# A fused attention and two-layer expert kernel: converting the second layers' weights two steps behind their load, every fourth step

## The chip, the cores and the metric

The kernel runs on one core of one Trainium2 chip. The metric is device time in microseconds (us) of one execution. The core has TensorE (PE, with its weight loads shown as PEld), VectorE (DVE), ScalarE (ACT), GpSimd (POOL) and SyncE (SP), which issues the DMAs. Each engine works through its own queue in order, so an instruction that waits holds up all that is queued behind it on that engine.

## The reference

Everything is computed in fp32.

```python
q_s = softmax(q, axis=-1); k_s = softmax(k, axis=2)        # 8 x 8 heads, 576 tokens, 64 wide
x = q_s @ (k_s.T @ v)                                      # per head, then heads side by side: 4608 x 512
h = x @ moe_w_in;  g = maximum(0.01 * h, h)                # 512 -> 2048
x = g @ moe_w_out                                          # 2048 -> 512
h = maximum(maximum(x @ w1, x @ w2), x @ w3)               # 512 -> 768
out = h @ moe2_w_out                                       # 768 -> 512
```

The weights arrive as 64-bit floats, seen by the kernel as pairs of 32-bit words; the attention inputs are 32-bit.

## The kernel before

Each fp32 product is made of three TensorE products of halves: every operand is split into a high part `hi` (rounded to the fast matmul type) and a rest `lo`, and `mm3` (line 334) adds hi x hi, hi x lo and lo x hi.

**Layer A.** The 4608 tokens are nine chunks of 512. For each chunk the 2048 hidden columns are worked in 16 pieces of 128; one piece of one chunk is a *step*, and there are 144 of them (chunks 0 and 1 are interleaved in turns). A step is `project` (12 products of 128x512 into a PSUM tile `ps`), then on ACT the Prelu of line 433 into a tile `g`, the ACT copy of line 351 into `ghi`, the DVE subtraction of line 352 into `glo`, and, one step later, `a_out`: 12 products that add to four accumulators `acc`. In the order of TensorE's queue a step's `a_out` stands behind the next step's `project`. So a step has 24 products. At the end of a chunk the accumulators are copied out (lines 358 and 360) into tiles of the same ring of three as `g`, and stored by DMA as `x`.

**Work in the background.** Between a step's `g` and the `a_out` of the step before, `background(step)` advances generators by one piece each: those that make k-transposed-times-v and the softmax of q for later chunks (`kv_unit`, `q_unit`; chunks 2 and 3 in an "early" form with TensorE transposes, later ones in another), and 24 *ahead units* that prepare layer B's weights. An ahead unit loads one 128 x 512 piece of 64-bit weights into a tile `room` (line 135), turns it into high and low 32-bit halves (`split_words`, lines 104 to 112: two ACT and seven DVE instructions, through a tile `ca`), and stores the result in a DRAM tensor `wb` (line 137). In the last chunk `weights_ready` (line 141) loads the prepared weights, and layer B begins after the 144 steps.

**Buffers and order.** `room` comes from the ring of 17 buffers of which 16 hold layer A's weights from the moment that the last of them is converted: one buffer is left, so that the load of a unit can only be issued when the store of the unit before has landed. The code gives the ahead units their steps (the first at step 48, one every third step), but that is a priority only: the framework draws up each engine's queue when the kernel is built, by playing the program through with its own estimates of all durations, and takes an instruction as early as its inputs and its buffer are there in that play. What it drew up is then the fixed order of each queue on the chip.

Of the kernel before, what the change touches and what calls it, by code (L numbers as in the profile page):

```python
# [13 lines left out]
AF = mybir.ActivationFunctionType  # L14
# [6 lines left out]
N = 512  # L21
# [17 lines left out]
def tile_kernel(ctx: ExitStack, tc: tile.TileContext, q, k, v, wa, wb, out):  # L39
# [12 lines left out]
    nc = tc.nc  # L52
# [6 lines left out]
    MA = wa.shape[0]  # L59
# [31 lines left out]
    x2 = {t: dp.tile([P, KDM, N], F32, name=f"x2_{i}") for i, t in enumerate(turns)}  # L91


    def split_words(raw, hi, lo, n):

        if raw.dtype != I64:
            nc.scalar.activation(hi, raw, AF.Copy)
            nc.vector.tensor_tensor(lo, raw, hi.bitcast(F32), op=ALU.subtract)
            return
        words = raw.bitcast(U32).rearrange("p (n t) -> p n t", t=2)  # L100
        high, low = words[:, :, 1], words[:, :, 0]
        a = cp.tile([P, 2 * N], U32, tag="ca", name="ca")[:, :n]
        af, bf = a.bitcast(F32), high.bitcast(F32)
        nc.scalar.activation(af, bf, AF.Abs)  # L104
        nc.vector.tensor_scalar(af, af, MOST_HIGH, LEAST_HIGH, op0=ALU.min, op1=ALU.max)  # L105
        nc.vector.tensor_scalar(a, a, 3, 0x3FFFFFF8, op0=ALU.logical_shift_left, op1=ALU.bitwise_and)
        nc.vector.scalar_tensor_tensor(a, high, 0xC0000000, a, op0=ALU.bitwise_and, op1=ALU.bitwise_or)  # L107
        nc.scalar.activation(hi, af, AF.Copy)
        nc.vector.tensor_scalar(high, a, 0xFF800000, None, op0=ALU.bitwise_and)  # L109
        nc.vector.scalar_tensor_tensor(bf, low, 2.0**-52, bf, op0=ALU.mult, op1=ALU.mult)  # L110
        nc.vector.tensor_tensor(af, af, hi.bitcast(F32), op=ALU.subtract)  # L111
        nc.vector.tensor_tensor(lo, af, bf, op=ALU.add)  # L112
# [7 lines left out]
    def weights(src):  # L120

        w = wp.tile([P, 2, 2, N], F32R, tag="w", name="w")
        raw = wp.tile([P, 2 * N], src.dtype, tag="w", name="raw")
        nc.sync.dma_start(raw, flat(src))
        split_words(raw, flat(w[:, 0]), flat(w[:, 1]), 2 * N)
        return parts(w)
# [1 line left out]

    ready = [[dp.tile([P, 2, 2, N], F32, name=f"wb{m}{i}") for i in range(2)] for m in range(MB)]

    def split_ahead(m, i, s):
        room = wp.tile([P, 4 * N], F32, tag="w", name="room")
        raw = room[:, 2 * N :].bitcast(wb.dtype)[:, :N]
        both = room[:, : 2 * N].bitcast(F32R).rearrange("p (t n) -> p t n", t=2)
        nc.sync.dma_start(raw, wb[m, i, :, s])
        split_words(raw, both[:, 0], both[:, 1], N)
        nc.sync.dma_start(ready[m][i][:, :, s], both.bitcast(F32))

    def weights_ready(m, i):
        w = wp.tile([P, 2, 2, N], F32R, tag="w", name="w")  # L140
        nc.sync.dma_start(w.bitcast(F32), ready[m][i])
        return parts(w)
# [85 lines left out]
    def x_tiles(c):  # L228
        if c not in xT:
            xT[c] = [xp.tile([P, KDM, N], F32R, tag=t, name=t) for t in ("xhi", "xlo")]  # L230
        return xT[c]
# [107 lines left out]
    def project(wslot, xpair):  # L339
        acc = psum()  # L340
        for kk in range(KDM):
            mm3(acc, cols(wslot, kk), tuple(t[:, kk] for t in xpair), kk == 0, kk == KDM - 1)
        return acc

    def f32_tile():
        return gp.tile([P, N], F32, tag="g", name="g", bufs=3)

    def split_g(g):
        hi = gp.tile([P, N], F32R, tag="ghi", name="ghi")
        lo = gp.tile([P, N], F32R, tag="glo", name="glo")  # L350
        nc.scalar.activation(hi, g, AF.Copy)  # L351
        nc.vector.tensor_tensor(lo, g, hi.bitcast(F32), op=ALU.subtract)  # L352
        return hi, lo
# [14 lines left out]
    def a_out(turn, m, gpair):  # L368
        c, first, last = turn[0], turn[1], turn[2] - 1
        if m == first:  # L370
            new_accs(c)
        for f in range(KDM):
            mm3(accs[c][f], cols(wA[m][1], f), gpair, m == first, m == last)
            if m == last:
                store(f, x2[turn][:, f], accs[c][f])


    def conv_a(m):
        wA[m] = weights(wa[m])
# [22 lines left out]
        yield  # L402

    def ahead_units():
        first = 3 * MA
        for j in range(4 * MB):
            yield first + 3 * j, ahead_unit(j // 4, j // 2 % 2, j % 2)

    def ahead_unit(m, i, s):
        split_ahead(m, i, s)  # L410
        yield

    waiting = [u for c in range(2, NC) for u in plan_units(c)] + list(ahead_units())
    waiting.sort(key=lambda u: u[0])
    live = []

    def background(step):
        while waiting and waiting[0][0] <= step:
            live.append(waiting.pop(0)[1])
        live[:] = [u for u in live if next(u, StopIteration) is not StopIteration]  # L420
# [7 lines left out]
    for turn in turns:  # L428
        c = turn[0]
        for m in range(*turn[1:]):  # L430
            acc = project(wA[m][0], x_tiles(c))
            g = f32_tile()
            nc.scalar.activation(g, acc, AF.Prelu, alpha=0.01)  # L433
            gpair = split_g(g)
            if c == 0 and m + LEAD < MA:
                conv_a(m + LEAD)
            background(step)
            if prev is not None:
                a_out(*prev)
            prev = (turn, m, gpair)  # L440
            step += 1
            if c == NC - 1 and m >= 2 and m - 2 < 2 * MB:
                wB.setdefault((m - 2) // 2, []).extend(weights_ready((m - 2) // 2, m % 2))
# [38 lines left out]
    for c in range(NC):  # L482
        for m in range(MB):
            accs3 = [project(wB[m][j], cur) for j in range(3)]
            g = f32_tile()
# [80 lines left out]
```

## Time and profile before

| | |
|---|---|
| median of 3 runs | 1544.13 us (1542.84 to 1545.41) |
| the profiled execution's own time | 1542.97 us |
| its span, first to last instruction | 1541.2 us |
| TensorE busy, weight loads busy | 1480.8 us (96%), 1209.4 us (78%) |
| VectorE, ScalarE, GpSimd busy | 716.4 us (46%), 456.3 us (30%), 34.8 us (2%) |

The span is some 2 us shorter than the time of the execution. Matmuls overlap, and their ends are modelled, so that the busy share of TensorE hides gaps of less than some 0.15 us; the number of 128x512 products done in a stretch tells more. Layer A's steps lie between 71.8 and some 947 us of the span, layer B behind that.

### The profile page before, as it was taken

The page shows a single profiled execution, that of the slowest core. Times are in us where ns is not written, and L with a number is a line of the kernel's source. Part 1 is how long each engine was busy: PE and PEld are TensorE (multiplying, and loading weights), DVE is VectorE, ACT ScalarE, POOL GpSimd, SP SyncE. Part 2 cuts the span into 40 slices and gives each one's busy share as a digit, 9 for nine tenths or more (in the row PEclk, how much of TensorE's full clock was granted, in tenths as well). Part 3 has the DMA queues.
Part 4 walks back from the last instruction along what each step waited for, and adds up shares of the span by engine and source line. Part 5 has one row for each costly group of instructions (what it writes and reads, how often), then busy time and mean ns, then how long its engine had stood idle before and what let it go on. Part 6 is the DMA issues. An engine that isn't in the chain of part 4 may idle for free.

```text
span 1541.2 us, 17524 instructions
## 1 busy us (share of the span) xinstructions
PE 1480.8 (96%) x7028; PEld 1209.4 (78%) x7028; DVE 716.4 (46%) x1348; ACT 456.3 (30%) x785; POOL 34.8 (2%) x50
## 2 busy tenths in 40 slices
PE   4799989999999999999999999999999999999998
PEld 3588868777777778888888887888888888888886
DVE  7989855558777764554421116122222222212121
ACT  4645544434343333333222223111121111111111
POOL 1100000000000000000000000000000000000000
PEclk8799999999999999999999999999999999999999
DMA  9055343333324232120000457010110101000000
GB/s 367 1 164 191 124 151 112 128 125 111 125 92 157 79 117 69 31 76 16 15 28 31 137 195 258 8 55 10 46 55 0 55 1 55 13 16 28 1 28 28
DMA packets 44481, 127.13 MB, mean 82 GB/s; under 512 B 4592, under 2 KB 4592, under 8 KB 38896
## 3 DMA queue, kind: packets, MB, share of 16 engines
q1 hardware_dynamic: 44400, 126.01, 23.8%
q8 instruction: 55, 0.90, 0.3%
q14 instruction: 26, 0.21, 0.1%
HBM read 88.24 MB, written 37.75 MB: 82 GB/s over the span
## 4 chain that ended last, share of the span: by engine, by line
PE 72%; DMA 12%; DVE 12%; issue 2%; ACT 2%; SPq 0%; POOL 0%; DVEq 0%; ACTq 0%
PE ps L334 44%; PE acc L334 26%; DMA room<-in_wb_dram 5%; DMA wb<-room 4%; DMA x<-g 1%; DVE ca L111 1%; DVE glo L352 1%; DVE ca L107 1%; ACT ca L104 1%; DVE room L112 1%; PE ps L313 1%; DVE qmx L268 1%; DVE ca L105 1%; DVE room L110 1%; DVE room L109 0%
## 5 line engine op out<-in xcount | busy, mean ns | idle before, releaser
L334 PE MATMUL ps<-xhi,w 128*128 128x512 f32 x2448 | 780.3, 391 | 4.8 <-ACT g L433 3.2
L334 PEld LDWEIGHTS ps<-xhi,w 128*128 128x128 f32 x2448 | 461.0, 188 | 102.3 <-ACT g L433 3.6
L334 PE MATMUL ps<-xlo,w 128*128 128x512 f32 x1224 | 477.6, 390 | 0.0
L334 PE MATMUL acc<-ghi,w 128*128 128x512 f32 x1152 | 387.0, 396 | 8.3 <-ACT ghi L351 3.8
L334 PEld LDWEIGHTS ps<-xlo,w 128*128 128x128 f32 x1224 | 230.9, 189 | 48.3 <-issue 0.2
L334 PEld LDWEIGHTS acc<-ghi,w 128*128 128x128 f32 x1152 | 215.6, 188 | 58.9 <-ACT ghi L351 8.2
L352 DVE TENSOR_TENSOR glo<-g,ghi 128x512 fp32r<-128x512 f32 x198 | 137.9, 696 | 226.1 <-ACT ghi L351 225.3
L334 PE MATMUL acc<-glo,w 128*128 128x512 f32 x576 | 226.8, 394 | 6.0 <-DVE glo L352 5.9
L351 ACT ACTIVATE ghi<-g 128x512 fp32r<-128x512 f32 x198 | 124.7, 630 | 225.6 <-DVE g L488 212.3
L487 DVE TENSOR_TENSOR g<-g,ps 128x512 f32<-128x512 f32 x54 | 37.2, 688 | 289.8 <-PE ps L334 289.8
L433 ACT ACTIVATE g<-ps 128x512 f32<-128x512 f32 x144 | 85.5, 595 | 276.6 <-PE ps L334 245.6
L334 PEld LDWEIGHTS acc<-glo,w 128*128 128x128 f32 x576 | 108.5, 188 | 33.1 <-DVE glo L352 11.4
L334 PE MATMUL acc<-w,ghi 128*128 128x512 f32 x432 | 132.5, 389 | 0.0
L334 PEld LDWEIGHTS acc<-w,ghi 128*128 128x128 f32 x432 | 81.0, 188 | 16.7
L486 ACT ACTIVATE g<-ps 128x512 f32<-128x512 f32 x54 | 32.3, 598 | 187.7 <-PE ps L334 185.9
L488 DVE TENSOR_TENSOR g<-g,ps 128x512 f32<-128x512 f32 x54 | 37.1, 688 | 103.3 <-PE ps L334 103.2
L334 PE MATMUL acc<-w,glo 128*128 128x512 f32 x216 | 83.5, 389 | 0.0
L105 DVE TENSOR_SCALAR ca<-ca 128x512 f32<-128x512 f32 (+1 forms) x40 | 21.2, 531 | 89.9 <-ACT ca L104 89.9
L360 ACT ACTIVATE g<-acc 128x512 f32<-128x512 f32 x48 | 28.3, 596 | 72.4 <-PE acc L334 68.7
L358 DVE COPY g<-acc 128x512 f32<-128x512 f32 x48 | 33.0, 688 | 33.9 <-DMA x<-g 16.8
L104 ACT ACTIVATE ca<-room 128x512 f32<-128x512 f32 x24 | 15.9, 662 | 110.6 <-DMA room<-in_wb_dram 110.5
L334 PEld LDWEIGHTS acc<-w,glo 128*128 128x128 f32 x216 | 40.6, 188 | 8.6
(97 smaller groups left out, 921.4 us busy)
## 6 DMA issues: line engine op xcount, KB each, us to landing
raw<-in_wa_dram SPq DMA_DIRECT2D x16, 1024.0 KB, 7.8
x<-g SPq DMA_DIRECT2D x60, 256.0 KB, 2.9
room<-in_wb_dram SPq DMA_DIRECT2D x24, 512.0 KB, 3.9
wb<-room SPq DMA_DIRECT2D x24, 512.0 KB, 3.1
w<-wb SPq DMA_DIRECT2D x12, 1024.0 KB, 4.8
xf<-x SPq DMA_DIRECT2D x9, 1024.0 KB, 4.9
out_dram<-g SPq DMA_DIRECT2D x36, 256.0 KB, 2.0
vt<-in_v_dram SPq DMA_DIRECT2D x24, 325.0 KB, 3.9
```

Source lines behind the costliest of these rows:

```text
L104: nc.scalar.activation(af, bf, AF.Abs)
L105: nc.vector.tensor_scalar(af, af, MOST_HIGH, LEAST_HIGH, op0=ALU.min, op1=ALU.max)
L107: nc.vector.scalar_tensor_tensor(a, high, 0xC0000000, a, op0=ALU.bitwise_and, op1=ALU.bitwise_or)
L334: nc.tensor.matmul(acc, lhsT=l, rhs=r, start=first and i == 0, stop=last and i == 2)
L351: nc.scalar.activation(hi, g, AF.Copy)
L352: nc.vector.tensor_tensor(lo, g, hi.bitcast(F32), op=ALU.subtract)
L358: nc.vector.tensor_copy(st, acc)
L360: nc.scalar.activation(st, acc, AF.Copy)
L433: nc.scalar.activation(g, acc, AF.Prelu, alpha=0.01)
L486: nc.scalar.activation(g, accs3[0], AF.Copy)
L487: nc.vector.tensor_tensor(g, g, accs3[1], op=ALU.max)
L488: nc.vector.tensor_tensor(g, g, accs3[2], op=ALU.max)
```

## The change

An ahead unit is now spread over three background pieces: in the first it issues the load, in the second nothing, and in the third it converts and stores. The conversion begins with a new ACT instruction, a copy of one column of the newest `g` (that of the step in which the third piece falls) into `ca`, which the `Abs` of line 104 then overwrites. The `Abs` and all behind it thereby depend on that step's Prelu. The first unit starts at step 33 in place of 48, and a new one every fourth step in place of every third: loads have their places at steps 33, 37, ... 125, conversions at 35, 39, ... 127.

```diff
-    def split_words(raw, hi, lo, n):
+    def split_words(raw, hi, lo, n, after=None):
...
         af, bf = a.bitcast(F32), high.bitcast(F32)
+        if after is not None:
+            nc.scalar.activation(af[:, 0:1], after[:, 0:1], AF.Copy)
         nc.scalar.activation(af, bf, AF.Abs)
...
-    def split_ahead(m, i, s):
+    newest = {}
+
+    def ahead_unit(m, i, s):
+
         room = wp.tile([P, 4 * N], F32, tag="w", name="room")
         raw = room[:, 2 * N :].bitcast(wb.dtype)[:, :N]
         both = room[:, : 2 * N].bitcast(F32R).rearrange("p (t n) -> p t n", t=2)
         nc.sync.dma_start(raw, wb[m, i, :, s])
-        split_words(raw, both[:, 0], both[:, 1], N)
+        yield
+        yield
+        split_words(raw, both[:, 0], both[:, 1], N, after=newest["g"])
         nc.sync.dma_start(ready[m][i][:, :, s], both.bitcast(F32))
...
     def ahead_units():
-        first = 3 * MA
+        first = 2 * MA + 1
         for j in range(4 * MB):
-            yield first + 3 * j, ahead_unit(j // 4, j // 2 % 2, j % 2)
-
-    def ahead_unit(m, i, s):
-        split_ahead(m, i, s)
-        yield
+            yield first + 4 * j, ahead_unit(j // 4, j // 2 % 2, j % 2)
...
             gpair = split_g(g)
+            newest["g"] = g
```

## Rows read from the trace of the kernel before

**Rows 1.** Busy time of each engine, its share of the span, and its instructions.

```profile
PE 1480.8 (96%) x7028; PEld 1209.4 (78%) x7028; DVE 716.4 (46%) x1348; ACT 456.3 (30%) x785; POOL 34.8 (2%) x50
```

**Rows 2.** Three stretches of layer A: from:to and length (us), busy time and count of PE, PEld, DVE, ACT and POOL, granted TensorE clock, busy share of the DMA engines, GB/s.

```profile
199.19:378.98 179.79, 167.62 (x855) 134.38 (x855) 111.70 (x243) 73.77 (x137) 8.40 (x8) 0.98 0.38 126
378.98:563.97 184.99, 172.98 (x857) 136.05 (x856) 131.11 (x292) 70.51 (x128) 6.48 (x7) 0.99 0.36 118
563.97:681.71 117.74, 117.74 (x612) 98.12 (x611) 62.70 (x144) 41.98 (x75) 3.51 (x5) 1.00 0.18 56
```

**Rows 3.** The same stretches, line 334 alone (the 128x512 products): PE and PEld.

```profile
199.19:378.98 179.79, 152.98 (x632) 118.75 (x631) 0.98 0.38 126
378.98:563.97 184.99, 163.00 (x673) 125.07 (x672) 0.99 0.36 118
563.97:681.71 117.74, 110.29 (x480) 89.70 (x480) 1.00 0.18 56
```

**Rows 4.** Line 433 (the Prelu, one a step) before the first of these stretches: ACT busy and count.

```profile
0.00:199.18 199.18, 12.98 (x22) 0.92 0.47 167
```

**Rows 5.** Who waited for whom from 196 to 564 us: idle time in total, times, longest.

```profile
ACT ca L104 <- DMA room<-in_wb_dram: 110.5, 23, 10.8
DVE ca L105 <- ACT ca L104: 84.7, 22, 8.5
ACT room L108 <- DVE ca L107: 18.1, 12, 3.5
PEld acc L334 <- DVE glo L352: 11.0, 13, 2.1
```

**Rows 6.** The same from 564 to 682 us.

```profile
ACT g L433 <- PE ps L334: 58.7, 19, 4.2
```

**Rows 7.** ACT in order of time, 504 to 524 us: start, duration, instruction [idle before, and what ended it].

```profile
516.72 0.66 ACT L104 ACTIVATE ca<-room 128x512 f32<-128x512 f32 x1 [10.85 <-DMA room<-in_wb_dram]
517.28 0.58 ACT L433 ACTIVATE g<-ps 128x512 f32<-128x512 f32 x1
```

**Rows 8.** PE in order of time in the same place.

```profile
509.99 0.39 PE L334 MATMUL ps<-xhi,w 128*128 128x512 f32 x1
...
518.58 0.50 PE L334 MATMUL acc<-ghi,w 128*128 128x512 f32 x1 [1.02 <-ACT ghi L351]
520.87 0.50 PE L334 MATMUL acc<-glo,w 128*128 128x512 f32 x1 [1.79 <-DVE glo L352]
```

**Rows 9.** SP's queue in the same place: a store and the next unit's load.

```profile
507.29 0.52 SPq L137 DMA_DIRECT2D wb<-room  x1
512.52 0.34 SPq L135 DMA_DIRECT2D room<-in_wb_dram  x1
```

**Rows 10.** One step of an undisturbed stretch, ACT, DVE and PE in order of time (the two PE rows each begin an `a_out`).

```profile
809.19 0.60 ACT L433 ACTIVATE g<-ps 128x512 f32<-128x512 f32 x1 [4.18 <-PE ps L334]
809.82 0.63 ACT L351 ACTIVATE ghi<-g 128x512 fp32r<-128x512 f32 x1
810.49 0.69 DVE L352 TENSOR_TENSOR glo<-g,ghi 128x512 fp32r<-128x512 f32 x1 [4.75 <-ACT ghi L351]
809.22 1.07 PE L334 MATMUL acc<-ghi,w 128*128 128x512 f32 x4
814.66 1.07 PE L334 MATMUL acc<-ghi,w 128*128 128x512 f32 x4
```

**Rows 11.** The first and the last of three stretches with a lower granted clock in layer A behind 196 us (columns as in rows 2).

```profile
231.95:235.36 3.41, 3.41 (x10) 2.62 (x9) 3.41 (x7) 1.49 (x3) 0.00 (x0) 0.50 0.00 0
522.09:525.50 3.41, 3.41 (x9) 2.63 (x9) 3.36 (x8) 1.85 (x4) 0.67 (x1) 0.50 0.24 74
```

**Rows 12.** The conversions' instructions on `room` in the second stretch (DVE and ACT, busy and count), and from the groups by line the two DVE instructions there that touch `ca` alone (busy us, mean ns).

```profile
378.98:563.97 184.99, 37.59 (x60) 14.92 (x24) 0.99 0.36 118
L105 DVE TENSOR_SCALAR ca<-ca 128x512 f32<-128x512 f32 x12 | 5.1, 427 | 34.8 <-ACT ca L104 34.8
L106 DVE TENSOR_SCALAR ca<-ca 128x512 uint32<-128x512 uint32 x12 | 5.0, 418 | 0.2
```

**Rows 13.** The units' loads: ns min/median/max of the issue, first and last start in us; and issue to landing of the units' loads and stores together.

```profile
L135 SPq DMA_DIRECT2D room<-in_wb_dram x24: 327/336/342, 196.7 to 542.0; - x24
DMA to landing us min/median/max: 3.0/3.7/5.2
```

**Rows 14.** What SP's queue waited for, 196 to 564 us (total, times, longest).

```profile
SPq L137 <- DVE room L112: 163.9, 22, 11.8
SPq L135 <- DMA wb<-room: 56.3, 23, 4.7
```

**Rows 15.** Small ACT instructions, 196 to 370 us (busy us, mean ns | idle before).

```profile
L212 ACT ACTIVATE plain<-ps,rc 64x64 f32<-64x64 f32 x12 | 3.7, 305 | 2.7 <-DVE rc L208 2.6
L186 ACT ACTIVATE diag<-ident,nmx 128x128 f32<-128x128 f32 x5 | 2.0, 403 | 10.1 <-DVE nmx L185 10.1
```

**Rows 16.** Loads of the prepared weights (as rows 13).

```profile
L141 SPq DMA_DIRECT2D w<-wb x12: 319/319/335, 559.1 to 922.4; - x12
```

**Rows 17.** PE where a chunk ends (step 64) with a conversion in the way, and where one ends (step 80) without.

```profile
486.22 0.50 PE L334 MATMUL acc<-ghi,w 128*128 128x512 f32 x1 [1.53 <-ACT g L360]
489.41 0.50 PE L334 MATMUL acc<-ghi,w 128*128 128x512 f32 x1 [0.86 <-DVE g L358]
588.91 0.50 PE L334 MATMUL acc<-ghi,w 128*128 128x512 f32 x1
```

## Prediction

> **What bounds the kernel now.** I began with the busy times [rows 1]: TensorE 96%, no other engine half busy. So time can only come from places where TensorE does not run products at its best rate, and I looked for these. The table of 40 us slices pointed at the time from some 200 to 560 us, and I cut layer A there into three stretches [rows 2]. The reader is to see that in the third, which has the same kinds of background work but no weight conversion, TensorE is never idle, while in the two before it 12.2 and 12.0 us of idle time show. Since the ends of matmuls are modelled, products are the better measure [rows 3]: 480 in 117.74 us is 0.2453 us for one (5.89 us a step of 24, background included); 673 in 184.99 us is 0.2749.
>
> Next, the waits [rows 5]. ACT stood 110.5 us in 23 waits of the `Abs` of line 104 for the load of `room`, and DVE stood behind it. In the third stretch ACT waits for TensorE instead [rows 6], as it should. One place shows the mechanism. The store of one unit is issued at 507.29, the next load only at 512.52 [rows 9], since both use the one free buffer. ACT stands before `Abs` until 516.72, with the Prelu of a finished product in its queue behind it [rows 7]: that product's last matmul had started at 509.99 (so it was ready near 510.4), and the Prelu ran at 517.28, 6.9 us late. TensorE then waited for `ghi` and for `glo` [rows 8].
>
> How much of such lateness is hidden is read from an undisturbed step [rows 10]: Prelu at 809.19, `glo` done at 810.49 + 0.69 = 811.18. The `a_out` that begins at 809.22 is the step before's; this `glo` is used by the next, at 814.66. The slack is 3.5 us. 6.9 - 3.5 = 3.4 us should be lost, and the two waits in rows 8 with what precedes them agree (1.02 + 1.79 idle, more under the modelled ends). Three times the granted clock then fell to half, 1.2 GHz, for 3.41 us, each time after stalls like these [rows 11].
>
> **What there is to win.** Second stretch: 673/480 x 117.74 = 165.1 us at the third's rate, against 184.99: 19.9 us lost. First stretch: 632/480 x 117.74 = 155.0; its early units do more on TensorE, 167.62 - 152.98 = 14.6 us outside line 334 against 632/480 x (117.74 - 110.29) = 9.8, so 4.8 more [rows 2, 3]: 159.8 against 179.79, 20.0 us lost. If the early shape costs nothing more the loss is 24.8; if its cost is twice that, 15.1. Together 39.9 us (35 to 45), 1.66 for each of the 24 conversions. Clock included: three times 3.41 us at half speed is 5.1 of it.
>
> The Trainium skill (Perfetto Trace Analysis, Identifying the Most-Contended Engine) tells one to improve the engine of highest occupancy; the change takes nothing from TensorE, so by that alone the time stays at 1543, and it is third among the rivals. The same section wants TensorE judged by its weight-load share and not by matmul busy time: by that share the loss would be 179.79 x (1 - 0.747/0.833) + 184.99 x (1 - 0.735/0.833) = 40 us, with the shares worked out from rows 2, and the trace bears out this half of the rule.
>
> **The change, part by part.**
>
> *Load and conversion apart.* A unit's load still goes out as soon as the store before it has landed, in either kernel. What moves is the place of `Abs` in ACT's queue. Before, the planner put it where its own estimate had the load landed, and that came out early by up to 10.8 us [rows 5]. Now it stands behind the Prelu of steps 35, 39, ... 127. Is the load there by then? Loads run from 196.7 to 542.0 us, 24 of them, so the whole round of load, conversion and store took 345.3/23 = 15.0 us with ACT's stalls inside [rows 13]. Four steps take 4 x 5.89 = 23.5. The load has 8.5 us to spare. So the 110.5 us of waits should go, to below 5. The first load can go out near 196.7 as before and waits for its turn until step 35.
>
> *Where the conversions now are.* 22 Prelus ran before 199.18 us [rows 4], and conversions began there; now steps 22 to 35 have none, then one falls on every fourth step, to step 127 (about 850 us of the old trace). About half land behind 560 us, where none stood. The DVE part of one is (37.59 + 5.1 + 5.0)/12 = 4.0 us, the ACT part 14.92/12 = 1.24 [rows 12]. In the third stretch DVE works 62.70 of 117.74 us, 12.5 per four steps; with a conversion 16.5 of 23.5. ACT is emptier. Neither becomes the bound; the cover for these 4 us is DVE's idle time and the 3.5 us of slack. If the whole conversion stood ahead of a `glo` that is due, 4.0 + 0.66 for the `Abs` less 3.5 would be 1.2 us lost, 28 us over 24.
>
> *The added copy.* One column; no row has it. It costs at least nothing and at most what a 128-column ACT instruction takes, 0.40 us [rows 15], 9.7 us in all; I take 0.3, the 64-column row, as it is the nearest, 7 us of ACT time. It stands behind `ghi` in the code and ACT has time (41.98 of 117.74 us busy), so it costs the end nothing; ahead of `ghi` its 0.3 is within the slack. By the Trainium skill (ScalarE: Activation LUTs, What ACT_TABLE_LOAD costs) it would be an estimated 0.19 us, 4.5 us of ACT time; no run here shows it. It also reads `g`, but `glo` reads that tile later, so the ring of three is held no longer.
>
> *SP's queue.* Stores wait there for the conversion, 163.9 us, and loads for the store to land, 56.3 [rows 14]; loads of k, v and q and the stores of `x` queue behind. With `Abs` no longer late the first should shrink to a few us a unit; the second stays, at some 2.4 us a unit. What it covered cost TensorE nothing in the third stretch; I count zero.
>
> *The end of chunks.* Here a residue is likely. Conversions fall on steps 47, 63, 79, ... 127, each just ahead of a chunk's end, where accumulators must be copied out by the same ACT and DVE. At step 64 with a conversion in the way TensorE waited 1.53 + 0.86 = 2.4 us; at step 80 without one, not visibly [rows 17]. Part of the 2.4 is again a late load. For six ends it is between 0 and 14.3 us; I take half, 7.
>
> *The deadline.* The prepared weights were loaded between 559.1 and 922.4 us, one early, the others in the last chunk [rows 16]. The last conversion now comes at about 850, so only that first load is late, and layer B needs it near 950. Nothing lost; a chain some 90 us later would be needed.
>
> **Sum.** The profiled execution took 1542.97 us (1.8 beyond its span, 1.2 below the median of 1544.13): 1543.0 - 39.9 + 7 = 1510, some 1511 as a median.
>
> **Rivals.**
>
> 1. *Forecast: the waits go, little comes in their place.* Between 1502 (39.9 won and nothing given back, on the median) and 1518 (twice the residue). For it: the third stretch with its slack and the 8.5 us of margin. 0.62.
>
> 2. *Half is given back.* Lateness moves from ACT's wait for the load into the queues: ACT waited 18.1 us before line 108 for DVE, up to 3.5 at once, and TensorE's weight loads 11.0 us for `glo` [rows 5]. These belong to a conversion among other background work, loaded in time or not. At half of 1.66 us each, 24 x 0.83 = 20 us: 1524, from 1518 to 1536. Against it: steps behind 560 us have more room on DVE. 0.21.
>
> 3. *No change.* The conversions cost what they cost wherever they are, or SP's waits still make the loads late: 24 x 1.66 remain, 1543 to 1544. Against it: rows 7 and 8 trace a loss to the load alone. 0.06.
>
> 4. *Slower.* One mechanism, in step 35 and each fourth one behind it: ACT stands before line 108 with the next Prelu behind, while DVE does the conversion ahead of `glo`. 4.0 + 1.24 + 1.5 (18.1/12, the mean wait) - 3.5 = 3.2 us a unit, 78 in all: 1543 - 40 + 78 = 1581. It decides from 1.66 us a unit. The planner would have to order all 24 badly; in the third stretch it ordered the same units without loss. 0.09.
>
> The 0.02 left are other things, on either side of none.
>
> **Numbers.** 0.2% is 3.1 us, about what a measurement of this kernel can tell from no change. Faster: cases 1 and 2 and a little, 0.85; same 0.06; slower 0.09. The range for 8 in 10 is 1500 to 1532: all of case 1, with the larger 45 us of loss at its low end, and most of case 2. The likeliest's own is 1502 to 1518.
>
> **What would show it.** In the new profile the wait of `Abs` for the load is gone from the list; line 104 on `room` runs from about 270 to 820 us; products in the first two stretches come at some 0.25 us each; no fall of the clock between 200 and 560 us. Wrong would be: new waits of ACT before line 108 or of TensorE for `glo` that sum to over 20 us, TensorE idle in the steps behind 560, or line 104 still waiting for its DMA.

## The result, and the profile after

The changed kernel took 1518.69 us (median of 4, 1517.31 to 1518.88) against 1543.49 for the kernel before in the same job (4, 1542.32 to 1545.41): ratio 0.9836, 95% interval 0.9819 to 0.9853, so 24.8 us faster. The forecast was 1511. The time lies in the range of 1500 to 1532, but 8 us above the point and just outside the likeliest case's own range, which ended at 1518. The profiled execution took 1517.31, with a span of 1515.2 us against 1541.2 before: 26.0 us to explain.

Lines shift in the new code: the products of line 334 are now on L344, `ghi` and `glo` on L361 and L362, the step's Prelu on L439, a conversion on L108 (the added copy), L109 (`Abs`) and L110 to L117, the units' load and store on L143 and L147, the loads of `ke` and `vt` on L180 and L182.

Busy times first, as [rows 1]:

```profile
PE 1471.1 (97%) x7028; PEld 1209.3 (80%) x7028; DVE 723.3 (48%) x1348; ACT 460.7 (30%) x809; POOL 34.7 (2%) x50
```

The work is the same but for 24 more ACT instructions, the copies. PE's busy time fell by 9.7 us at the same count of matmuls; the weight loads, which [rows 1] gives as 1209.4, did not move, only their share of the shorter span did.

Who waited for whom, the whole stretch in which conversions now run, 196 to 860 us (total us, times, longest; the largest groups that concern a conversion):

```profile
ACT room L113 <- DVE ca L112: 59.2, 24, 4.5
DVE mx L204 <- DMA ke<-in_k_dram: 30.7, 14, 4.3
PEld acc L344 <- DVE glo L362: 5.3, 4, 2.9
PE acc L344 <- DVE glo L362: 3.7, 3, 2.5
```

The first row of [rows 5], `Abs` behind the load of `room` with 110.5 us, has no answer: no such wait is left. ACT now stands before the next conversion line for DVE in all 24 units (59.2 us; 18.1 in 12 units before), and DVE's waits for the load of `ke` have grown from 9.9 us in 9 waits to 30.7 in 14. SP's queue, to hold against [rows 14]:

```profile
SPq L147 <- DVE room L117: 339.7, 24, 19.0
SPq L143 <- DMA wb<-room: 49.8, 23, 4.4
```

Three stretches to hold against [rows 2] and [rows 3] (columns as there). The first two run from the same step to the same step as there; all engines for these. Then L344 alone for all three, the third cut between two products, so that it holds the same 480 as the third of [rows 3]:

```profile
200.67:366.58 165.91, 161.80 (x850) 131.61 (x849) 83.83 (x191) 64.87 (x124) 9.92 (x8) 1.00 0.24 80
366.58:536.79 170.21, 167.69 (x862) 138.60 (x861) 115.78 (x254) 67.17 (x126) 4.92 (x7) 0.99 0.30 96
```

```profile
200.67:366.58 165.91, 147.85 (x628) 116.02 (x627) 1.00 0.24 80
366.58:536.79 170.21, 157.85 (x678) 127.35 (x676) 0.99 0.30 96
538.18:656.15 117.97, 110.56 (x480) 89.64 (x480) 1.00 0.31 99
```

Divide length by products, as the prediction did with [rows 3]. First stretch: 0.2845 us before, 165.91/628 = 0.2642 now. Second: 0.2749 before, 170.21/678 = 0.2511 now. Third: 0.2453 before, 117.97/480 = 0.2458 now. With before's counts the gain is 632 x 0.0203 = 12.8 us in the first stretch and 673 x 0.0238 = 16.0 in the second, and the third gives back 480 x 0.0005 = 0.2. (The start-up ahead of step 22 is 1.5 us longer here: 200.67 against 199.18; 201.71 in another kernel below, which has the same work there.) Those four make 27.1 us by the end of the third stretch, of which some 1 us is lost behind it in small places, down to the 26.0 of the spans. The forecast was 20.0 and 19.9, less 7 for the ends of chunks. The first stretch falls 7.2 us short; the second falls 3.9 short, and that is to be held against the 7.

One conversion in ACT's order of time (start, duration, instruction [idle before, and what ended it]):

```profile
409.07 0.58 ACT L439 ACTIVATE g<-ps 128x512 f32<-128x512 f32 x1
409.68 0.63 ACT L361 ACTIVATE ghi<-g 128x512 fp32r<-128x512 f32 x1
410.22 0.19 ACT L108 ACTIVATE ca<-g 128x1 f32<-128x1 f32 x1
410.44 0.67 ACT L109 ACTIVATE ca<-room 128x512 f32<-128x512 f32 x1
414.01 0.63 ACT L113 ACTIVATE room<-ca 128x512 fp32r<-128x512 f32 x1 [2.91 <-DVE ca L112]
414.55 0.58 ACT L439 ACTIVATE g<-ps 128x512 f32<-128x512 f32 x1
```

The copy and the `Abs` stand directly behind `ghi`, nothing waits for a load, and ACT's 2.91 us wait for DVE hardly holds up the next Prelu: the last matmul of its product ended near 414.2, some 0.4 us before it started. This is what [rows 7] looked like without the 10.85.

What is left in the second stretch is one place (a smaller stall, 0.97 us before a `glo` at 358.51, lies just ahead of it). SP's queue, DVE and PE near 380 us:

```profile
372.66 0.33 SPq L143 DMA_DIRECT2D room<-in_wb_dram  x1
373.67 0.45 SPq L180 DMA_DIRECT2D ke<-in_k_dram  x1
```

```profile
380.53 1.30 DVE L204 TENSOR_REDUCE mx<-ke 128x128 f32<-128x640 f32 x1 [4.25 <-DMA ke<-in_k_dram]
384.72 0.68 DVE L362 TENSOR_TENSOR glo<-g,ghi 128x512 fp32r<-128x512 f32 x1
```

```profile
385.46 0.79 PE L344 MATMUL acc<-glo,w 128*128 128x512 f32 x1 [2.52 <-DVE glo L362]
```

The load of `ke` was issued at 373.67, 1.0 us behind a unit's load, and DVE could begin on it only at 380.53, 4.25 us of which it stood idle. The `glo` that TensorE needed stood behind that instruction in DVE's queue, and TensorE waited 2.52 us for it. The clock then was at 0.50, 1.2 GHz:

```profile
385.41:388.82 3.41, 3.36 (x8) 2.68 (x9) 3.12 (x10) 1.96 (x5) 0.00 (x0) 0.50 0.00 0
```

### The profile page after: what moved, and what is told of

Same layout as the page of the kernel before. It is cut to its first block, busy times and chain, and to the rows that moved or that the text cites. A ratio compares the mean times of both kernels' runs of the same rounds, so it can differ in the third digit from the quotient of the medians.

```text
span 1515.2 us, 17548 instructions
## 1 busy us (share of the span) xinstructions
PE 1471.1 (97%) x7028; PEld 1209.3 (80%) x7028; DVE 723.3 (48%) x1348; ACT 460.7 (30%) x809; POOL 34.7 (2%) x50
## 4 chain that ended last, share of the span: by engine, by line
PE 87%; DVE 6%; DMA 5%; issue 1%; ACT 1%; SPq 0%; POOL 0%; POOLq 0%; DVEq 0%; ACTq 0%
PE ps L344 51%; PE acc L344 32%; DMA ke<-in_k_dram 2%; PE ps L214 1%; PE ps L323 1%; DMA x<-g 1%; PE ps L305 1%; DMA raw<-in_wa_dram 1%; DVE qsm L284 0%; DVE qmx L278 0%; DMA qt<-in_q_dram 0%; DMA part<-x 0%; PE ps L296 0%; DMA spare<-in_v_dram 0%; DVE qo L275 0%
## 5 line engine op out<-in xcount | busy, mean ns | idle before, releaser
L344 PE MATMUL ps<-xhi,w 128*128 128x512 f32 x2448 | 776.4, 389 | 4.6 <-DVE xlo L330 2.5
L344 PEld LDWEIGHTS ps<-xhi,w 128*128 128x128 f32 x2448 | 459.6, 188 | 101.2 <-DVE xlo L330 2.9
L344 PE MATMUL ps<-xlo,w 128*128 128x512 f32 x1224 | 476.2, 389 | 0.0
L344 PE MATMUL acc<-ghi,w 128*128 128x512 f32 x1152 | 384.2, 394 | 0.7 <-ACT ghi L361 0.7
L344 PEld LDWEIGHTS ps<-xlo,w 128*128 128x128 f32 x1224 | 229.9, 188 | 47.9 <-issue 0.2
L344 PEld LDWEIGHTS acc<-ghi,w 128*128 128x128 f32 x1152 | 216.3, 188 | 46.9 <-ACT ghi L361 1.1
L362 DVE TENSOR_TENSOR glo<-g,ghi 128x512 fp32r<-128x512 f32 x198 | 137.8, 696 | 201.8 <-ACT ghi L361 201.3
L344 PE MATMUL acc<-glo,w 128*128 128x512 f32 x576 | 226.3, 393 | 4.2 <-DVE glo L362 4.2
L361 ACT ACTIVATE ghi<-g 128x512 fp32r<-128x512 f32 x198 | 124.9, 631 | 226.6 <-DVE g L495 212.3
L439 ACT ACTIVATE g<-ps 128x512 f32<-128x512 f32 x144 | 85.5, 594 | 297.4 <-PE ps L344 257.5
L344 PE MATMUL acc<-w,ghi 128*128 128x512 f32 x432 | 132.5, 389 | 0.0
L344 PEld LDWEIGHTS acc<-glo,w 128*128 128x128 f32 x576 | 108.7, 189 | 28.2 <-DVE glo L362 6.3
L344 PEld LDWEIGHTS acc<-w,ghi 128*128 128x128 f32 x432 | 81.1, 188 | 16.7
L344 PE MATMUL acc<-w,glo 128*128 128x512 f32 x216 | 83.5, 389 | 0.0
L344 PEld LDWEIGHTS acc<-w,glo 128*128 128x128 f32 x216 | 40.6, 188 | 8.4
L204 DVE TENSOR_REDUCE mx<-ke 128x128 f32<-128x640 f32 x16 | 21.0, 1311 | 30.7 <-DMA ke<-in_k_dram 30.7
L330 DVE TENSOR_TENSOR xlo<-ps,xhi 128x512 fp32r<-128x512 f32 x36 | 24.4, 682 | 21.7 <-ACT xhi L329 21.7
```

Source lines behind the costliest of these rows:

```text
L204: nc.vector.tensor_reduce(mx, ke.rearrange("p r d -> p d r"), axis=AX.X, op=ALU.max)
L330: nc.vector.tensor_tensor(xlo[:, hp], xps, xhi[:, hp].bitcast(F32), op=ALU.subtract)
L344: nc.tensor.matmul(acc, lhsT=l, rhs=r, start=first and i == 0, stop=last and i == 2)
```

## The experiments

Two things were to be told apart at first: which half of the change does the work (the spacing of the units, or the data dependence that ties a conversion to a Prelu), and whether the time that did not come back was the conversions' own cost. Later ones followed the misses. The diffs are against the changed kernel unless said otherwise.

**Spacing alone.** The copy that makes the dependence is left out; units are still loaded at step 33 + 4j and converted two steps on in program order.

```diff
-        split_words(raw, both[:, 0], both[:, 1], N, after=newest["g"])
+        split_words(raw, both[:, 0], both[:, 1], N)
```

> The changed kernel without the one-column copy: units start at step 33, one every fourth step, conversion two pieces behind the load, but nothing ties a conversion to a step's Prelu. Theory A (what counts is where Abs stands in ACT's queue, and only the dependence moves it): the planner takes conversions as early as the one free buffer allows, as before, so 1543 us, within 3, with some 110 us of ACT waiting for the load of room. Theory B (what counts is that the units are spread out in the code): some 1519 us, as with the change.

1542.66 us against 1544.46; ratio 0.9985 (0.9974 to 0.9996). ACT's wait is that of [rows 5] again:

```profile
ACT ca L109 <- DMA room<-in_wb_dram: 108.8, 23, 10.8
```

The planner put the instructions of every engine in the same order as in the kernel before. So the place in the program, and the pause of two steps, decide nothing here: the planner moves a conversion as early as its own estimate of the load allows, and only the dependence holds it back.

**The dependence alone.** Units again start at step 48, one every third step, load and conversion in one piece, as before the change; the copy stays.

```diff
-        yield
-        yield
         split_words(raw, both[:, 0], both[:, 1], N, after=newest["g"])
...
+        yield
...
-        first = 2 * MA + 1
+        first = 3 * MA
...
-            yield first + 4 * j, ahead_unit(j // 4, j // 2 % 2, j % 2)
+            yield first + 3 * j, ahead_unit(j // 4, j // 2 % 2, j % 2)
```

> The kernel before with the one-column copy alone: units at steps 48, 51, ... 117, load and conversion in one piece, each conversion tied to the Prelu of its own step. Theory A: three steps are 17.7 us against a round of 15.0 or less, so the load still lands first; ACT waits under 10 us in all for it, and the time is that of the change or a little better, 1512 to 1521 us, since steps 33 to 48 have no conversion. Theory B (two steps of distance and every fourth step are needed): loads come late again in part, 1525 to 1543 us.

1513.85 us (ratio 0.9801, 0.9782 to 0.9819), and the wait:

```profile
ACT ca L109 <- DMA room<-in_wb_dram: 7.4, 5, 3.1
```

One copy of one column, in an otherwise old arrangement, takes 103.1 of the 110.5 us of waiting away and gives the whole gain of the change, by medians 4.8 us more.

**Half the distance between units.** A unit every second step in place of every fourth.

```diff
-            yield first + 4 * j, ahead_unit(j // 4, j // 2 % 2, j % 2)
+            yield first + 2 * j, ahead_unit(j // 4, j // 2 % 2, j % 2)
```

> The changed kernel with a unit every second step in place of every fourth (steps 33, 35, ... 79; conversions asked for at 35, 37, ... 81, each tied to its step's Prelu). Two steps are 11.8 us, less than the round of load, conversion and store through the one buffer (15.0 us with stalls, some 12 to 14 without). Theory A: the dependence no longer decides, the buffer does, and Abs again stands in ACT's queue ahead of its load: ACT waits for the load some 60 to 110 us in all, and the time is 1530 to 1545 us. If the dependence on g by itself were the cure, some 1519 us.

1544.27 us, ratio 1.0005 (0.9991 to 1.0018): all of the gain gone.

```profile
ACT ca L109 <- DMA room<-in_wb_dram: 87.3, 23, 8.7
PEld acc L344 <- DVE glo L362: 17.7, 20, 2.1
```

Two steps are some 11.8 us, and a round of load, conversion and store through the one free buffer needs about 15 [rows 13]; the conversion is tied to its Prelu, its load still is not there, and the next Prelu stands behind it. The dependence helps only as long as the round fits.

**Every third step.** The distance between the two.

```diff
-            yield first + 4 * j, ahead_unit(j // 4, j // 2 % 2, j % 2)
+            yield first + 3 * j, ahead_unit(j // 4, j // 2 % 2, j % 2)
```

> The changed kernel with a unit every third step (33, 36, ... 102; conversions at 35 to 104). Three steps are 17.7 us against a round of 12 to 15: the load is still in time, and ACT's wait for it stays under 10 us. 1516 to 1524 us; the denser conversions next to the early units may cost a few us. If it comes out above 1530, the margin of the buffer's round was judged too wide.

1521.23 us, ratio 0.9856 (0.984 to 0.9872). **And every third from step 49**, sixteen later:

```diff
-        first = 2 * MA + 1
+        first = 3 * MA + 1
...
-            yield first + 4 * j, ahead_unit(j // 4, j // 2 % 2, j % 2)
+            yield first + 3 * j, ahead_unit(j // 4, j // 2 % 2, j % 2)
```

> The changed kernel with units at steps 49, 52, ... 118 (conversions at 51 to 120): none among the early units of chunk 3, and denser behind. The trace of the changed kernel shows some 2 us lost between steps 35 and 48 with four conversions, and 3.9 us between 48 and 77, of which one stall near 385 us is the most. If conversions among early units cost, 1512 to 1517 us; if the residue is the early units' own work, 1517 to 1521 us.

1511.60 us, ratio 0.9793 (0.9779 to 0.9808). `Abs` waits for its load 8.9 us in all in the first and 4.7 in the second, so three steps (17.7 us) are enough for a round. The two differ in something else. DVE's wait for `ke` in the second stretch (366 to 540 us), every third from 33, then from 49:

```profile
DVE mx L204 <- DMA ke<-in_k_dram: 14.4, 5, 4.2
```

```profile
DVE mx L204 <- DMA ke<-in_k_dram: 6.4, 6, 1.4
```

The slower one has waits of up to 4.2 us, as the changed kernel had at 380, the faster one none above 1.4. But the largest single stall of the slower one, at 472 us, comes from other transfers in the same queue: a chunk's stores of `x` stood behind a unit's load, DVE waited for them, and TensorE for DVE.

```profile
DVE g L368 <- DMA x<-g: 7.8, 1, 7.8
PE acc L344 <- DVE g L368: 2.5, 1, 2.5
```

The reason given for the expectation of the faster one, conversions among the early units, is not borne out: those at 37, 41, ... (below) fall among them too and are as fast.

**More work in a conversion.** Six more DVE instructions of 128x512 (each a maximum of the low part with itself) in every conversion.

```diff
+        for _ in range(6):
+            nc.vector.tensor_tensor(both[:, 1], both[:, 1].bitcast(F32), both[:, 1].bitcast(F32), op=ALU.max)
```

> The changed kernel with six more DVE instructions of 128x512 at the end of each conversion (some 0.69 us each, 4.1 us a unit, 99 us of DVE work in all), which leave the result as it is. If a conversion behind step 48 is fully covered by DVE's idle time (12.5 + 4.0 of 23.5 us per four steps, then 20.6), the time grows by less than 6 us, to 1519 to 1525. If DVE's queue is already at the edge (rival 2 of the prediction, half given back), each added us costs at least half: over 1550 us.

1520.17 us, ratio 0.9846 (0.9826 to 0.9866), 1.5 us above the changed kernel: less than the two intervals can tell apart. The second stretch:

```profile
368.64:537.35 168.71, 167.23 (x862) 136.92 (x861) 144.82 (x307) 67.40 (x128) 4.92 (x7) 1.00 0.29 95
```

29.0 us more of DVE work than in the changed kernel (144.82 against 115.78), for the same 862 matmuls in 1.5 us less. The two do not differ in work alone, though: the stall of 2.52 us that the changed kernel has at 385 is not in this one, where a matmul waits 1.3 us for `glo` at the longest. So the rate is held against that of a kernel without any units (0.2438 us a product, below). Line 346 is the products' here:

```profile
368.64:537.35 168.71, 157.39 (x678) 125.66 (x676) 1.00 0.29 95
```

168.71/678 = 0.2488, so 678 x 0.0050 = 3.4 us are lost in this stretch with 29.0 us of DVE work added, where the changed kernel loses 4.9 without it. A conversion that does not wait for its load is hidden but for little, with room for as much again.

**No conversion.** The kernel before, with each unit reduced to a load and a store of 512 KB.

```diff
-        raw = room[:, 2 * N :].bitcast(wb.dtype)[:, :N]
-        both = room[:, : 2 * N].bitcast(F32R).rearrange("p (t n) -> p t n", t=2)
-        nc.sync.dma_start(raw, wb[m, i, :, s])
-        split_words(raw, both[:, 0], both[:, 1], N)
-        nc.sync.dma_start(ready[m][i][:, :, s], both.bitcast(F32))
+        both = room[:, : 2 * N].rearrange("p (t n) -> p t n", t=2)
+        nc.sync.dma_start(both, x2[turns[0]][:, :2])
+        nc.sync.dma_start(ready[m][i][:, :, s], both)
```

> The kernel before with the nine conversion instructions of the 24 units left out: a unit loads a piece of the same size (512 KB of the first x tile, in place of the weights) and stores it, so that layer B works on other numbers. This gives the floor that ahead units can be brought down to. The prediction had 39.9 us lost to conversions, 20.0 of them between steps 22 and 48: by it the time is some 1503 us. The rival, from the trace of the changed kernel, where steps 22 to 35 have no conversion and still take 80.5 us for 297 products (some 5.6 us more than the clean rate with the early units' own extra): about a third of the first stretch's 20.0 belongs to the early units themselves, and the floor is 1511 to 1515 us, only some 4 to 7 below the changed kernel.

1540.23 us, ratio 0.9972 (0.9962 to 0.9983): a miss for every expectation. With nothing between load and store the planner packed all 24 units into the first half of what they took before, 7.5 us apart, and another wait took the place of ACT's. The units' loads (as [rows 13]), the waits of DVE and of SP's queue, and the first two stretches:

```profile
L134 SPq DMA_DIRECT2D room<-x x24: 319/328/335, 198.3 to 369.8; - x24
```

```profile
DVE qmx L266 <- DMA qt<-in_q_dram: 37.5, 13, 11.8
DVE mx L192 <- DMA ke<-in_k_dram: 23.0, 9, 11.4
SPq L135 <- DMA room<-x: 78.3, 24, 4.4
```

```profile
200.80:392.62 191.82, 166.69 (x832) 132.59 (x830) 71.30 (x160) 59.05 (x111) 8.15 (x8) 0.95 0.54 187
392.62:562.45 169.83, 169.68 (x878) 140.83 (x879) 89.39 (x208) 59.03 (x105) 4.92 (x7) 1.00 0.16 51
```

SP stood 78.3 us before stores whose load had not landed; loads of q and k stood behind them in the queue, and DVE waited up to 11.8 us for one. That load of q went out at 230.31, where a kernel without units (below) issues it at 224.68; and the loads of q in this stretch took 5.2 us to land (median) against 3.1 there. Which of the two, the late issue or the slower landing, weighs more, no run parts. The loss is in the first stretch alone (25.1 us without a matmul, granted clock 0.95) and is gone in the second, where no units are left. So this is not the floor that it was meant to be; it shows that the units' DMAs in SP's queue, which the prediction counted at zero, can cost nearly as much as ACT's waits: 29.5 us over the kernel without units.

**No units at all.** The kernel before without the 24 units; the prepared weights of layer B are taken from the first tile of x instead.

```diff
-        nc.sync.dma_start(w.bitcast(F32), ready[m][i])
+        nc.sync.dma_start(w.bitcast(F32), x2[turns[0]].rearrange("p (t s) n -> p t s n", t=2))
...
-    waiting = [u for c in range(2, NC) for u in plan_units(c)] + list(ahead_units())
+    waiting = [u for c in range(2, NC) for u in plan_units(c)]
```

> The kernel before without the 24 ahead units at all (no load, conversion or store of layer B's weights); layer B loads tensors of the same shape that hold the first x tile, so its numbers are others. This is the floor for anything done with the units. By the prediction's sum (39.9 us lost to them) 1503 us. By the traces so far (stretches without conversions in the changed kernel still lose some 6 us to the early units; the run with units converted in the step of their load's place, at 33, 37, ..., came to 1510.8) the floor is 1508 to 1513 us.

1510.73 us against 1545.02, ratio 0.9781 (0.976 to 0.9801). This is the floor: all that units can cost, load, conversion, store and waits, is 34.3 us. Its first two stretches, all engines; the same, line 334 alone; and DVE and PE near 230 us:

```profile
201.71:363.66 161.95, 158.66 (x831) 129.27 (x830) 72.58 (x164) 59.80 (x111) 7.87 (x8) 0.99 0.19 66
363.66:533.33 169.67, 169.67 (x880) 140.98 (x879) 88.50 (x204) 59.04 (x104) 4.91 (x7) 1.00 0.17 51
```

```profile
201.71:363.66 161.95, 144.71 (x609) 113.68 (x608) 0.99 0.19 66
363.66:533.33 169.67, 159.83 (x696) 129.73 (x694) 1.00 0.17 51
```

```profile
227.36 0.69 DVE L268 TENSOR_REDUCE qmx<-qt 128x8 f32<-128x512 f32 x1 [5.75 <-DMA qt<-in_q_dram]
```

```profile
230.91 0.80 PE L334 MATMUL ps<-xhi,w 128*128 128x512 f32 x1 [2.60 <-DVE xlo L320]
```

The second stretch runs at 169.67/696 = 0.2438 us a product, a little better than the third of before. The first runs at 161.95/609 = 0.2659 though no unit is in it, with TensorE standing 2.60 us for `xlo` at 230.91 and a mean granted clock of 0.57 in the 3.41 us behind it. What stood ahead of that `xlo` on DVE was again a wait for a load, 5.75 us for a tile of q. The first of the dips of [rows 11], at 231.95, stands at the same place of the kernel before, so a conversion is not needed for it. Nor does the dip come each time: the changed kernel has the same wait, and its clock stayed up.

```profile
229.83 0.50 PE L344 MATMUL ps<-xhi,w 128*128 128x512 f32 x1 [2.45 <-DVE xlo L330]
```

```profile
229.83:233.24 3.41, 3.41 (x16) 2.78 (x17) 2.48 (x5) 1.45 (x4) 1.04 (x1) 1.00 0.00 0
```

**No pause, other steps.** Load and conversion in one piece behind the Prelu of steps 33, 37, ... 125.

```diff
         nc.sync.dma_start(raw, wb[m, i, :, s])
-        yield
-        yield
         split_words(raw, both[:, 0], both[:, 1], N, after=newest["g"])
         nc.sync.dma_start(ready[m][i][:, :, s], both.bitcast(F32))
+        yield
```

> The changed kernel with load and conversion in one piece (no two steps between them): loads at steps 33, 37, ..., conversions tied to the Prelu of the same step. Since the load goes out as soon as the store before it has landed, wherever it stands in the code, the two steps of distance should do nothing: 1516 to 1522 us, no wait for the load. If the distance is needed, loads are late: over 1530 us.

1510.81 us, ratio 0.9788 (0.9773 to 0.9802): better than expected by 5 us or more. This changed two things at once, the pause and the steps on which conversions fall (33 in place of 35), so two more kernels part them. **The pause kept, the steps moved by two** (conversions at 37, 41, ... 129):

```diff
-        first = 2 * MA + 1
+        first = 2 * MA + 3
```

> The changed kernel, two steps of distance kept, with the first unit at step 35 in place of 33: conversions at 37, 41, ... 129, the places modulo four of the run without distance that was 7.9 us faster than the change. If it is the place that counts (there the unit's store and the next load go out some 10 us ahead of ke and vt, here in the changed kernel 1 to 3 us ahead of them, and ke lands in 3.5 against 5.0 us), 1509 to 1514 us. If it is the distance that costs, some 1519 us.

1511.09 us, ratio 0.979 (0.977 to 0.9809). **The pause taken out, the steps kept** (conversions at 35, 39, ... 127):

```diff
-        yield
-        yield
         split_words(raw, both[:, 0], both[:, 1], N, after=newest["g"])
         nc.sync.dma_start(ready[m][i][:, :, s], both.bitcast(F32))
+        yield
...
-        first = 2 * MA + 1
+        first = 2 * MA + 3
```

> Load and conversion in one piece, first unit at step 35: conversions at 35, 39, ... 127 as in the changed kernel, without the two steps of distance. If the place counts and not the distance, 1516 to 1521 us, as the changed kernel; if the distance costs, 1509 to 1513 us.

1518.90 us, ratio 0.9837 (0.982 to 0.9853). Every engine's instructions stand in the same order as in the changed kernel, and TensorE's stall is back at the same place, with its clock:

```profile
387.30:390.80 3.50, 3.48 (x9) 2.82 (x10) 3.23 (x10) 1.94 (x5) 0.00 (x0) 0.58 0.00 0
```

So "two steps behind its load" does nothing; on which steps the conversions fall, 35, 39, ... or 33 or 37, 41, ..., is worth some 8 us. A reason shows in SP's queue. In the changed kernel, and then in the one with conversions at 33, 37, ..., one unit's load and the load of a chunk's `ke`:

```profile
419.67 0.33 SPq L143 DMA_DIRECT2D room<-in_wb_dram  x1
421.56 0.33 SPq L180 DMA_DIRECT2D ke<-in_k_dram  x1
```

```profile
404.95 0.33 SPq L143 DMA_DIRECT2D room<-in_wb_dram  x1
414.76 0.43 SPq L179 DMA_DIRECT2D ke<-in_k_dram  x1
```

The unit's load goes out 1.9 us ahead of `ke` in the one and 9.8 in the other. The `ke` loads between 366 and 662 us, what waited for them and how long they took from issue to landing, in the changed kernel and then with conversions at 37, 41, ...:

```profile
  DMA ke<-in_k_dram: 27.2, 12
DMA to landing us min/median/max: 4.4/5.0/6.8
```

```profile
  DMA ke<-in_k_dram: 4.2, 6
DMA to landing us min/median/max: 3.2/3.5/5.0
```

Without any units the median is 3.5 as well. No run moves these loads alone, and with the steps the order of ACT's and DVE's instructions changes too; that the loads are the reason is read from the traces and not shown by a run of its own.

The second stretch of the kernel with conversions at 37, 41, ... has the conversions in it (DVE 113.28 us) and runs at 167.95/689 = 0.2438 us a product, exactly the rate without any units:

```profile
365.37:533.32 167.95, 167.95 (x873) 139.56 (x872) 113.28 (x258) 66.95 (x127) 8.13 (x7) 1.00 0.30 97
```

```profile
365.37:533.32 167.95, 158.11 (x689) 128.31 (x687) 1.00 0.30 97
```

That version is faster than both kernels, 7.6 us below the changed one by medians, and stands at the floor; so does the one without the pause from step 33.

## Why the prediction was right, and where it was 8 us off

**The mechanism was right.** The loss was a load late in ACT's queue. Take the dependence out of the change and 108.8 us of waiting and 1543 us are back; put it alone into the old arrangement and both are gone. By the Trainium skill's rule on the engine of highest occupancy (Perfetto Trace Analysis, Identifying the Most-Contended Engine), nothing should have come of it, as the prediction read it, since TensorE's work is untouched; 24.8 us came, out of gaps that a late instruction on ACT had opened on TensorE itself. The same section's measure, the share of weight loads, is borne out again: it rose from 78% [rows 1] to 80% while the loads' busy time stayed.

**The margin of the load was right.** A round of 15.0 us, four steps of 23.5: no wait at four steps, 8.9 us of it at three, 87.3 at two, where the gain is gone.

**Hidden conversions: right, for the reason given.** A stretch with 29.0 us more DVE work lost 3.4 us against the rate without units. Rival 2, half given back to queues of ACT and DVE, fails as a mechanism, though the time, 1518.69, lies at the lower edge of its range of 1518 to 1536 and outside the forecast case's own. Rival 4's mechanism does occur (ACT before L113 for DVE, 59.2/24 = 2.5 us a unit) but behind `ghi`, in time that ACT has: the Prelu behind it starts at most 2.0 us after its product's last matmul, within the slack of 3.5. Rival 3 fails.

**The added copy** took 0.185 to 0.187 us in all 24, where 0.3 was taken; the Trainium skill's estimate of 0.19 (ScalarE: Activation LUTs, What ACT_TABLE_LOAD costs) was nearer, and the time hangs on neither.

**The term that failed: the 20.0 us of the first stretch.** The prediction took 4.8 us off for what the early units do on TensorE, and let it go to twice that; it counted only their busy time outside line 334. Without any units that stretch still loses 161.95 - 609 x 0.2453 = 12.6 us against the third's rate. Of these, work outside the line is 158.66 - 144.71 - 609 x 7.45/480 = 4.5, as forecast; but TensorE also stands 161.95 - 158.66 = 3.3 us idle, and the products themselves are busy 144.71 - 609 x 110.29/480 = 4.8 us longer, with the low clock behind the wait for `xlo` among it. Both were put down to the conversions. With 12.6 x 632/609 = 13.0 in place of 4.8, the working's own sum gives 24.8 - 13.0 = 11.8 us, outside its bounds of 15.1 to 24.8. That is the difference of the two kernels' rates, 632 x (0.2845 - 0.2659). The term was 8.2 us too large, about the whole miss. (The profiled execution of the changed kernel did a little better there, 12.8, since its clock stayed up behind the wait for `xlo`.)

**The 19.9 us of the second stretch** were right: 673 x (0.2749 - 0.2438) = 20.9 against the kernel without units. The two terms then make 32.7, where taking all units away won 30.9 us of span and 34.3 of median.

**The residue: right in size by luck, wrong in kind.** 7 us were set down for six chunk ends with a conversion in the way. The changed kernel is 8.0 us above the floor by medians, 4.9 by the spans of the two profiled executions, and 678 x (0.2511 - 0.2438) = 4.9 of that is the second stretch, which has one visible stall. That one does come behind a chunk's end, but through a late load: a unit's load 1.0 us ahead of `ke`, DVE standing before `ke`, `glo` behind it. This was the step "SP's queue, I count zero". Moved steps remove it, and the packed units of the kernel without conversions show the same queue with 25.1 us without a matmul. The other 3 us of the medians are mostly the choice of execution: the profiled one of the changed kernel was the fastest of its four (1517.31, the next 1518.51), that of the kernel without units the slowest of its four (1512.04, median 1510.73).

**Wrong with little effect:** the stores' wait in SP's queue was to shrink from 163.9 us and rose to 339.7, because a landed load now waits for its turn, and its store with it. And the clock was to fall nowhere between 200 and 560 us; it fell behind the stall at 385, which is in the residue. The low end of the forecast case, 1502, does not come out of its own terms either: 1544.1 - 39.9 is 1504.

So the forecast of 1510 becomes, with the one term put right, 1543 - 11.8 - 19.9 + 7 = 1518.

## What to carry to other kernels

Where a planner fixes the order of an engine's queue by its own estimate of a load, moving an instruction in the program may do nothing at all; a data dependence on work that is surely later, here a copy of one column for 0.19 us, moves it, and it helps as long as the buffer's round fits between two units. When a loss is read as "this stretch against a clean one", first ask what else differs between the two: a kernel with the suspect taken out gives the floor for one run, and here it would have shown that 13 us of the first stretch belonged to other work. And a unit that is hidden on every engine still has DMAs: look at what stands next to them in the issuing queue, for the steps on which they fell were worth 8 us here.

## What the runs showed of the hardware

A load of `ke` took 5.0 us (median, up to 6.8) from issue to landing in the changed kernel, where a unit's load had gone out 1 to 3 us ahead of it, and 3.5 where that was 7 to 11 us ahead (conversions at 37, 41, ...) or where there were no units. The Trainium skill says that DMAs run on the same 16 engines and interleave whichever engine starts them (DMA: Bandwidth & Descriptors, Issuing engines are not separate DMA queues); the slower landing agrees with the interleaving, though all of these are started by SP and the page gives no such duration. A single stall of TensorE can be dearer than it looks, but need not be. Behind the one of 2.52 us at 385.46 the granted clock stood at 0.50, 1.2 GHz, for 3.41 us, with 3.36 us of busy time there; behind the one of 2.45 us at 229.83 in the same trace it stayed at 1.00.
